# A planner's order placed anew, and two scan-kernel sums in one PSUM bank: an S4 layer with a feed-forward gate

## The chip, the cores and the metric

The kernel runs on one core of a Trainium2 chip. The core has a matrix engine (TensorE, PE in the views, with its weight loads as PEld), a vector engine (VectorE, DVE), a scalar engine (ScalarE, ACT), GpSimd (POOL) and SyncE (SP), which issues most of the transfers. Each runs its own instructions in program order; a semaphore holds an instruction until what it needs is there. SBUF is the on-chip memory, PSUM the banks into which PE accumulates, 2 KB per partition each. The metric is the time of one execution on the device in microseconds; the time before is the median of three runs.

## The reference

Both branches work on the normalised input; the result is the input plus their product. L is 2048, D 512, the state has 128 entries, and the hidden layer F is 1792 wide.

```python
xn = layernorm(u)
# branch A: an S4 convolution
logdA = dt * (A_re + 1j * A_im); dB = dt * (B_re + 1j * B_im)
P = exp(logdA[:, :, None] * arange(L))
K = einsum("dn,dnl,dn->dl", Cc, P, dB).real          # the scan kernel, 512 x 2048
y = irfft(rfft(pad(xn.T)) * rfft(pad(K)))[:, :L].T + xn * Dskip
# branch B: a feed-forward layer
g = silu(gelu(xn @ w1 + b1) @ w2 + b2)
out = u + y * g
```

## The kernel before

**Two stages.** The first, called the projection stage here, builds the scan kernel K and runs the feed-forward layer at the same time; in the trace it lasts from the start to about 392 us. The second does the convolution as small Fourier transforms written as matmuls, multiplies by the gate and adds the input. Only the first stage's code and order are touched.

**The feed-forward work.** The 2048 rows are four blocks of 512; the 14 tiles of the hidden layer are taken in two halves, so there are 56 steps j of one block and one tile. Each fp32 product is three matmuls, high times high, high times low and low times high. Per step: `F` is the first layer (two halves of six 128x512 matmuls, L250 to L252), `G` the gelu on ACT (L264), `H` the cast to the high part on ACT (L270), `R` the subtraction that gives the low part `hl` on DVE (L276), `S` the second layer (four parts of three matmuls, L289 to L291). `W`, `WB` load weights and `WS` splits them in high and low parts (ACT L233, DVE or POOL L235; the low part of the first layer's weight is `w1l`). For the later blocks the rows are normalised and turned here as well: `LS` and `LR` are statistics, `LC` the scaling of two row groups (DVE, L345), `TF` the transposes on PE (L361), `TH` and `TL` the split of the transposed rows into `xh` and `xl` (the latter on DVE, L376).

**The scan kernel.** K is built in 32 sets of 16 channels. Per set s: `KL` loads its numbers, `A` computes the phases (one bf16 matmul each for two halves, L593, into the `ph` bank), `B` rounds them to whole turns, on ACT (L601) or DVE (L603) as a flag in the order says, `C` takes the turns off (DVE, L607), `N` makes sines (ACT, L627 to L630), `Z` the sizes (POOL, a chain of seven operations, L616 to L621), `E` multiplies sizes and sines to the tables e1 and e2 (DVE, three steps: L642, L646, L648 and L649), `Q` sums over the state (64 fp32 matmuls of 128x32 by 128x64 in PE's records, L657), `U` copies the sum out of PSUM (ACT, L663), and `UD` stores it to DRAM (SP). `P` steps through the parameters that the sets need. The sums have one PSUM bank, tag `sm`, half filled. The tables have two buffers each.

**What sets the order.** `ORDER` (L48 to L128) is a string of tokens such as `F.24.0` or `E.11.2`; the kernel walks it from the first to the last and calls the function that the table `acts` (L735) names for each. Since the engines run in program order, the string fixes the order on every engine and every queue, and so which work stands ahead of a waiting instruction. The gelu and the sine need different tables in ACT, so an ACT_TABLE_LOAD stands wherever the string changes from the one to the other.

Of the kernel before, what the change touches and what calls it, by code (L numbers as in the profile page):

```python
# [48 lines left out]
WS.0.3 LD.0 LD.1 P.0 WS.1.0 WS.1.1 P.0 P.0 WS.1.2 G.0 F.1.0 LS.2.0 W.2 LS.3.1 H.0 R.0 WB.2 S.0.0 P.0  # L49
S.0.1 LS.3.0 LL.4 WS.1.3 P.0 WS.2.0 LL.5 W.3 F.1.1 WS.2.1 WB.3 S.0.2 LS.2.1 WS.2.2 G.1 WS.2.3 W.4 S.0.3  # L50
F.2.0 P.0 F.2.1 H.1 WS.3.0 R.1 WS.3.1 P.0 S.1.0 WS.3.2 WB.4 G.2 P.0 WS.4.0 S.1.1 W.5 WS.3.3 P.0 H.2
WS.4.1 P.0 WB.5 F.3.0 P.0 S.1.2 P.0 WS.4.2 LR.2 F.3.1 G.3 S.1.3 R.2 WS.5.0 WS.5.1 KL.0.0 F.4.0 WS.4.3.1
W.6 F.4.1 LC.2 H.3 LC.3 S.2.0 G.4 KL.0.1 TF.2.0 WB.6 BB A.0.0 TH.2.0 LS.5.0 R.3 S.2.1 KL.1.0 TF.2.1
LS.4.0 B.0.0.1 TH.2.1 TL.2.0 C.0.0 WS.6.0 S.2.2 S.2.3 H.4 TF.3.0 A.0.1 KL.1.1 WS.5.2 S.3.0 LS.5.1 WS.6.1
Z.0 B.0.1 P.0 P.1 TH.3.0 S.3.1 C.0.1 S.3.2 A.1.0 N.0.0 TL.2.1 S.3.3 KL.2.0 LD.2 TL.3.0 WS.6.2 B.1.0.1
C.1.0 R.4 F.5.0 TF.3.1 Z.1 LD.3 LS.4.1 N.0.1 A.1.1 B.1.1.1 F.5.1 S.4.0 WS.5.3.1 TH.3.1.1 C.1.1 G.5 S.4.1
E.0.0 S.4.2 S.4.3 E.0.1 TL.3.1 F.6.0 H.5 N.1.0 R.5 F.6.1 LR.4 N.1.1 F.7.0 E.0.2 G.6 A.2.0 B.2.0.1 S.5.0
KL.2.1 LC.5 H.6 F.7.1 S.5.1 P.1 LC.4 C.2.0 WS.6.3 LK.0 F.8.0 S.5.2 A.2.1 G.7 KL.3.0 H.7 B.2.1 P.1 F.8.1
R.6 G.8 KL.3.1 C.2.1 N.2.0 S.5.3 F.9.0 E.1.0 N.2.1 Q.0 A.3.0 S.6.0 S.6.1 S.6.2 F.9.1 Z.2 E.1.1 R.7 U.0
E.1.2 P.1 LD.5 B.3.0.1 LD.4 C.3.0 O.0.0 TF.4.0 KL.4.0 Q.1 Z.3 O.0.1 H.8 S.6.3 TH.4.0 O.0.3 G.9 A.3.1  # L60
S.7.0 TL.4.0 B.3.1.1 P.1 H.9 S.7.1 C.3.1 O.0.2 KL.4.1 TF.4.1 UD.0 LL.6 TH.4.1 R.8 F.10.0 F.10.1 E.2.0
S.7.2 S.7.3 N.3.0 E.2.1 A.4.0 TL.4.1 P.1 S.8.0 R.9 KL.5.0 U.1 E.2.2 N.3.1 B.4.0.1 G.10 OK.0 S.8.1 F.11.0
E.3.0 F.11.1 S.8.2 C.4.0 A.4.1 S.8.3 Q.2 G.11 B.4.1 H.10 UD.1 TF.5.0 E.3.1 E.3.2 LK.1 F.12.0 H.11 TH.5.0
C.4.1 A.5.0 KL.6.0 LS.6.0 F.12.1 B.5.0.1 S.9.0 S.9.1 R.10 N.4.0 G.12 S.9.2 TL.5.0 TF.5.1 P.1 N.4.1 C.5.0
KL.5.1 S.9.3 F.13.0 A.5.1 U.2 TH.5.1 F.13.1 R.11 S.10.0 P.1 B.5.1 Z.4 P.1 P.1 Q.3 C.5.1 N.5.0 TL.5.1
S.10.1 P.1 E.4.0 P.1 UD.2 U.3 F.14.0 N.5.1 H.12 E.4.1 S.10.2 KL.6.1 UD.3 S.10.3 R.12 E.4.2 Z.5 G.13 A.6.0
S.11.0 S.11.1 F.14.1 H.13 LK.2 E.5.0 R.13 E.5.1 LL.7 S.11.2 S.11.3 B.6.0.1 C.6.0 Q.4 Z.6 S.12.0 G.14
A.6.1 KL.7.0 F.15.0 E.5.2 P.1 S.12.1 LS.7.0 B.6.1 LS.7.1 F.15.1 P.2 C.6.1 S.12.2 A.7.0 S.12.3 G.15 LS.6.1
F.16.0 B.7.0 C.7.0 LR.6 N.6.0 A.7.1 S.13.0 LC.6 KL.8.0 S.13.1 U.4 H.14 R.14 P.1 H.15 F.16.1 N.6.1 LC.7
P.2 UD.4 E.6.0 B.7.1 R.15 S.13.2 LD.6 KL.7.1 C.7.1 F.17.0 Z.7 S.13.3 F.17.1 G.16 TF.6.0 O.1.0 O.1.2 Q.5  # L70
A.8.0 E.6.1 G.17 TF.7.0 S.14.0 TH.6.0 P.2 TH.7.0 E.6.2 O.1.1 U.5 O.1.3 H.16 KL.8.1 TL.6.0 TL.7.0 B.8.0
N.7.0 Z.8 S.14.1 S.14.2 N.7.1 S.14.3 F.18.0 OK.1 UD.5 C.8.0 TF.6.1 A.8.1 P.2 Q.6 F.18.1 S.15.0 B.8.1.1
R.16 TH.6.1 S.15.1 C.8.1 S.15.2 U.6 KL.9.0 S.15.3 E.7.0 H.17 E.7.1 S.16.0 W.7 S.16.1 G.18 WB.7 A.9.0
KL.9.1 F.19.0 F.19.1 R.17 E.7.2 B.9.0 TL.6.1 N.8.0 S.16.2 W.8 LD.7 S.16.3 N.8.1 G.19 S.17.0 TF.7.1 C.9.0
A.9.1 E.8.0 P.2 H.18 KL.10.0 TH.7.1 E.8.1 Q.7 B.9.1.1 UD.6 C.9.1 KL.10.1 H.19 D S.17.1 S.17.2 A.10.0
E.8.2 S.17.3 N.9.0 WB.8 F.20.0 TL.7.1 P.2 F.20.1 U.7 KL.11.0 N.9.1 R.18 Z.9 B.10.0 S.18.0 C.10.0 E.9.0
A.10.1 Q.8 G.20 F.21.0 XL.0 W.9 S.18.1 B.10.1 C.10.1 KL.12.0 N.10.0 E.9.1 N.10.1 WB.9 S.18.2 E.9.2 R.19
S.18.3 W.10 F.21.1 A.11.0 F.22.0 U.8 B.11.0 C.11.0 S.19.0 KL.11.1 G.21 H.20 S.19.1 A.11.1 S.19.2 UD.7
Z.10 B.11.1 P.2 P.2 F.22.1 UD.8 LK.3 S.19.3 R.20 F.23.0 WB.10 G.22 C.11.1 E.10.0 N.11.0 S.20.0 Z.11
A.12.0 F.23.1 N.11.1 S.20.1 Q.9 H.21 O.2.0 S.20.2 E.10.1 E.10.2 B.12.0 KL.12.1 F.24.0 H.22 C.12.0 A.12.1  # L80
U.9 S.20.3 F.24.1 B.12.1 O.2.1 R.21 R.22 G.23 S.21.0 S.21.1 Q.10 KL.13.0 O.2.3 F.25.0 O.2.2 E.11.0 F.25.1
C.12.1 E.11.1 KL.13.1 S.21.2 N.12.0 P.2 Z.12 KL.14.0 G.24 UD.9 P.2 H.23 N.12.1 U.10 R.23 P.2 E.11.2
S.21.3 P.2 Z.13 E.12.0 S.22.0 S.22.1 H.24 E.12.1 F.26.0 P.2 A.13.0 B.13.0 WS.7.0 Q.11 S.22.2 G.25 R.24
UD.10 C.13.0 F.26.1 S.22.3 A.13.1 WS.7.1 S.23.0 B.13.1.1 S.23.1 WS.8.0 S.23.2 C.13.1 KL.14.1 WS.7.2.1
# [1122 lines left out]
```

## Time and profile before

| | |
|---|---|
| median of the runs | 548.25 us (547.44 to 548.85) |
| profiled execution | 548.29 us |
| its span | 546.5 us |
| granted TensorE clock, mean | 0.996 |
| busy PE, DVE, ACT, POOL | 526.9, 463.9, 394.5, 279.1 us |
| ACT_TABLE_LOAD, all lines | 66 in the program, 1283 ns each |
| sum copies L663, 32 | 11.6 us |

In the page, busy time is the time in which an engine had an instruction running; PE's starts are recorded, its ends are modelled, and overlapping matmuls start less than their duration apart. In a row of a timeline stand the start, the duration, the engine, the line, the operation with its output and inputs, and in brackets the idle time before it with what ended it. In a row of groups stand the count, the busy time in us, the mean duration in ns, and the idle time ahead of the group with what ended it.

### The profile page before, as it was taken

Reading aid. Unit: us, or ns where it says so; the run is one execution under the profiler, and the core shown is the slowest. Engines: PE = TensorE matmul, PEld = TensorE weight load, DVE = VectorE, ACT = ScalarE, POOL = GpSimd, SP = SyncE. Lnnn points to the kernel's source line nnn. Section 1 sums busy time; section 2 is a strip of 40 time slices with the busy share of each in tenths; the row PEclk is TensorE's granted clock in tenths of the full one; section 3 lists DMA queues with packets and bytes.
Section 4 is the critical chain, followed back from the end, with each engine's and each line's share of the span. In section 5 each row is a group of like instructions: output and inputs, shape, how many; then the busy total and the mean of one; then the engine's idle time right before and its main releaser. Section 6 shows DMA issues by size and latency. Waiting matters only on the chain.

```text
span 546.5 us, 16626 instructions
## 1 busy us (share of the span) xinstructions
PE 526.9 (96%) x6999; PEld 421.2 (77%) x6999; DVE 463.9 (85%) x736; ACT 394.5 (72%) x570; POOL 279.1 (51%) x385
## 2 busy tenths in 40 slices
PE   8898999999999999999999999999999999999993
PEld 7666787778776777777777777777789998997971
DVE  6899989999999889999888797789557688787896
ACT  3777998898987899959799777889664573652430
POOL 5648379358968559996854296356301001203031
PEclk9999999999999999999999999999999999999998
DMA  8937526744385172837038412913547749361562
GB/s 228 315 124 227 196 83 221 237 150 146 121 245 180 33 237 90 270 102 198 18 110 263 123 47 84 188 45 103 204 160 221 136 127 189 120 194 67 182 208 93
DMA packets 88391, 85.85 MB, mean 157 GB/s; under 512 B 42134, under 2 KB 65050, under 8 KB 87292
## 3 DMA queue, kind: packets, MB, share of 16 engines
q1 hardware_dynamic: 79248, 66.43, 41.6%
q0 software_dynamic: 8768, 17.83, 10.6%
q8 instruction: 55, 0.90, 0.7%
q10 hardware_dynamic: 300, 0.53, 0.3%
q14 instruction: 20, 0.16, 0.1%
HBM read 51.22 MB, written 33.55 MB: 155 GB/s over the span
## 4 chain that ended last, share of the span: by engine, by line
PE 76%; DVE 17%; issue 2%; ACT 1%; POOL 1%; DMA 1%; DVEq 0%; ACTq 0%; POOLq 0%
PE s L913 11%; PE z L289 8%; PE z L290 7%; PE z L291 7%; PE f L250 7%; PE f L252 7%; PE f L251 7%; PE s L891 6%; PE sa L949 6%; PE kg L657 5%; PE ph L593 2%; DVE hl L276 2%; DVE ra L607 2%; DVE e L646 1%; PE y L989 1%
## 5 line engine op out<-in xcount | busy, mean ns | idle before, releaser
L619 POOL TENSOR_TENSOR mm<-mm,rc 128x32 f32<-128x32 f32 (+4 forms) x150 | 115.4, 769 | 11.8
L289 PE MATMUL z<-w2h,hh 128*128 128x512 f32 x224 | 97.8, 437 | 0.0
L250 PE MATMUL f<-xh,w1h 128*128 128x512 f32 x220 | 91.4, 416 | 0.0
L291 PE MATMUL z<-w2h,hl 128*128 128x512 f32 x224 | 88.4, 395 | 0.3 <-DVE hl L276 0.3
L252 PE MATMUL f<-xh,w1l 128*128 128x512 f32 x220 | 87.1, 396 | 1.7 <-DVE w1l L235 1.7
L290 PE MATMUL z<-w2l,hh 128*128 128x512 f32 x224 | 88.6, 395 | 0.0
L251 PE MATMUL f<-xl,w1h 128*128 128x512 f32 x220 | 86.7, 394 | 0.0
L913 PE MATMUL s<-X,mc 64*64 64x128 f32 x1536 | 60.4, 273 | 0.2 <-issue 0.2
L930 DVE TENSOR_TENSOR t<-s,uh 128x512 f32<-128x512 f32 x64 | 41.0, 684 | 22.8 <-ACT uh L921 22.6
L276 DVE TENSOR_TENSOR hl<-hf,hh 128x512 fp32r<-128x512 f32 x56 | 52.9, 948 | 4.6 <-ACT hh L270 4.6
L616 POOL COPY mm<-rc 128x32 f32<-128x32 f32 x30 | 13.4, 446 | 77.7 <-DVE e L649 53.4
L264 ACT ACTIVATE hf<-f,b1s 128x512 f32<-128x512 f32 x56 | 38.2, 688 | 20.4 <-DVE hl L276 11.7
L252 PEld LDWEIGHTS f<-xh,w1l 128*128 128x128 f32 x220 | 41.3, 188 | 12.9 <-DVE w1l L235 3.0
L289 PEld LDWEIGHTS z<-w2h,hh 128*128 128x128 f32 x224 | 42.5, 190 | 10.5 <-issue 1.0
L291 PEld LDWEIGHTS z<-w2h,hl 128*128 128x128 f32 x224 | 42.1, 188 | 10.7 <-DVE hl L276 0.7
L607 DVE SCALAR_TENSOR_TENSOR ra<-ra,ph 128x512 f32<-128x512 f32 x64 | 43.6, 681 | 7.5 <-ACT ra L601 6.5
L913 PEld LDWEIGHTS s<-X,mc 64*64 64x64 f32 x1536 | 44.5, 133 | 5.8 <-issue 1.7
L290 PEld LDWEIGHTS z<-w2l,hh 128*128 128x128 f32 x224 | 42.3, 189 | 8.3 <-DVE w2l L235 0.2
L250 PEld LDWEIGHTS f<-xh,w1h 128*128 128x128 f32 x220 | 41.5, 189 | 9.2 <-ACT hf L264 0.2
L251 PEld LDWEIGHTS f<-xl,w1h 128*128 128x128 f32 x220 | 41.4, 188 | 9.0
L921 ACT COPY uh<-s 128x512 f32<-128x512 f32 x32 | 18.7, 586 | 38.3 <-PE s L913 18.4
L642 DVE TENSOR_TENSOR e<-mm,ra 128x1024 f32<-128x1024 f32 x32 | 42.0, 1311 | 4.7 <-POOL pr_h L524 2.4
(184 smaller groups left out, 1161.1 us busy)
## 6 DMA issues: line engine op xcount, KB each, us to landing
x<-in_A_u_dram SPq DMA_DIRECT2D x8, 512.0 KB
xs<-x SPq DMA_DIRECT2D x8, 512.0 KB
xt_h<-xh POOLq DMA_DIRECT2D x4, 1024.0 KB, 5.5
xt_l<-xl POOLq DMA_DIRECT2D x4, 1024.0 KB, 7.6
kgd<-ko SPq DMA_DIRECT2D x32, 128.0 KB
za<-zo SPq DMA_DIRECT2D x4, 1024.0 KB
xh<-xt_h POOLq DMA_DIRECT2D x4, 1024.0 KB, 6.1
xl<-xt_l POOLq DMA_DIRECT2D x4, 1024.0 KB, 10.1
```

Source lines behind the costliest of these rows:

```text
L250: PE.matmul(p, wh[:, k, :], xh[:, k, :], start=(k == 0), stop=False)
L251: PE.matmul(p, wh[:, k, :], xl[:, k, :], start=False, stop=False)
L252: PE.matmul(p, wl[:, k, :], xh[:, k, :], start=False, stop=(k == KD - 1))
L276: V.tensor_sub(hl, hf, hh)
L289: PE.matmul(z, hh[:, s], wh, start=(f0 == 0 and not rows), stop=False)
L290: PE.matmul(z, hh[:, s], wl, start=False, stop=False)
L291: PE.matmul(z, hl[:, s], wh, start=False, stop=(f0 == FA - 1))
L607: V.scalar_tensor_tensor(ra[:, 0, c], ra[:, 1, c], MAGIC, p, op0=ALU.subtract, op1=ALU.subtract)
L619: GP.tensor_mul(mv[:, :, 0:3:2, w:2 * w], mv[:, :, 0:3:2, 0:w], rc[:, 2 + 2 * i:4 + 2 * i, :].rearrange("p j c -> p c j").unsqueeze(3).to_ ...
L642: V.tensor_mul(e1, m1.unsqueeze(1).to_broadcast([P, 2, CH, N1]), ra[:, :, :, :N1])
L913: PE.matmul(p[ka * 64:(ka + 1) * 64, r, o, :, jj], w, xf[b][h, c, :, k, :], start=(c == 0), stop=(c == 1), skip_group_check=True)
L930: V.tensor_mul(t, p[:, i, :, 1].unsqueeze(1).to_broadcast([P, 2, 2, P]), uh)
```

## The change

**One.** `gen_sum` is called for odd s only. It takes a bank of the shape [P, 2, DD, N2], which is the whole of 2 KB per partition, and runs over the tables of set s − 1 and of set s in one go, 128 matmul records with nothing else between. `gen_out` copies 128x512 elements once, from one bank to one tile `ko` (one buffer of double size where there were two), and `gen_keep` stores 256 KB at once. There are 16 `Q`, `U` and `UD` steps where there were 32. The tables of the even set are held until the pair's sum has run; they still have two buffers.

**Two.** The string `ORDER` is written anew from beginning to end, 1250 tokens where it had 1298; the 48 fewer are the even `Q`, `U` and `UD`. The work is the same otherwise, with two differences: 40 of the 64 roundings run on ACT and 24 on DVE, where 29 and 35 did, and there are 55 changes of the ACT table in the program where there were 66. Line numbers of the changed kernel are lower by 2.

```diff
@@ ORDER: three places of the new string, then the same of the old
+S.3.0 S.3.1 A.0.1 WB.6 WS.5.0 S.3.2 S.3.3 WS.5.1 LC.3 TF.3.0 B.0.1 C.0.1 P.0 P.1 WS.4.3.1 WS.6.0 TH.3.0
...
+A.15.0 N.13.1 N.14.0 E.13.0 Z.14 U.11 E.13.1 E.13.2 B.15.0 C.15.0 UD.11 S.26.2 WB.11 W.12 Z.15 H.27 R.27
+S.26.3 F.28.1 N.14.1 Q.13 G.28 F.29.0 WS.10.0 A.15.1 WS.11.0 WS.9.2 F.29.1 E.14.0 S.27.0 WB.12 WS.10.1
...
+U.23 G.47 F.48.0 A.27.1 KL.29.0 Q.25 N.26.0 B.27.1.1 C.27.1 S.45.2 S.45.3 N.26.1 N.27.0 R.46 S.46.0
...
-W.6 F.4.1 LC.2 H.3 LC.3 S.2.0 G.4 KL.0.1 TF.2.0 WB.6 BB A.0.0 TH.2.0 LS.5.0 R.3 S.2.1 KL.1.0 TF.2.1
@@ gen_size
-            for n in range(2):
-                GP.memset(par.tile([P, DD, N2], F32, tag="ko", name=f"ko_{n}", bufs=2)[:, 0, :1], 0.0)
+            GP.memset(par.tile([P, 2, DD, N2], F32, tag="ko", name="ko_")[:, 0, 0, :1], 0.0)
@@ gen_sum, gen_out, gen_keep
     def gen_sum(s):
-        e1, e2 = gen[s]["e"]
-        p = pss.tile([P, DD, N2], F32, tag="sm", name=f"kg{s}")
-        for d in range(DD):
-            for c in range(2):
-                for g in range(G):
-                    PE.matmul(p[g * N1:(g + 1) * N1, d, :], e1[:, c, g * DD + d, :], e2[:, c, g * DD + d, :],
-                              start=(c == 0), stop=(c == 1), skip_group_check=True)
+        p = pss.tile([P, 2, DD, N2], F32, tag="sm", name=f"kg{s}")
+        for n in range(2):
+            e1, e2 = gen[s - 1 + n]["e"]
+            for d in range(DD):
+                for c in range(2):
+                    for g in range(G):
+                        PE.matmul(p[g * N1:(g + 1) * N1, n, d, :], e1[:, c, g * DD + d, :], e2[:, c, g * DD + d, :],
+                                  start=(c == 0), stop=(c == 1), skip_group_check=True)
         gen[s]["p"] = p
     def gen_out(s):
-        gen[s]["ko"] = ko = par.tile([P, DD, N2], F32, tag="ko", name=f"ko{s}", bufs=2)
+        gen[s]["ko"] = ko = par.tile([P, 2, DD, N2], F32, tag="ko", name=f"ko{s}")
         A.copy(ko, gen[s]["p"])
     def gen_keep(s):
-        b, j = divmod(s, SPB)
-        SY.dma_start(kgd[b][:, j * DD * N2:(j + 1) * DD * N2], gen.pop(s)["ko"].rearrange("p a b -> p (a b)"))
+        b, j = divmod(s // 2, SPB // 2)
+        SY.dma_start(kgd[b][:, j * 2 * DD * N2:(j + 1) * 2 * DD * N2], gen.pop(s)["ko"].rearrange("p n a b -> p (n a b)"))
```

**Three places of the order.** The first is on DVE early in the stage, where the rows of the second block are scaled; `x_228` holds four groups of rows, `hl` is the low part of a step of the feed-forward layer, `xl` that of the transposed rows. Before:

```order
L340 SCALAR_TENSOR_TENSOR rs_358<-t_543,rs_358 128x4
L276 TENSOR_TENSOR hl_2_563<-hf_2_486,hh_2_505 128x512
L345 TENSOR_SCALAR x_228<-x_228,mv_357,rs_358 128x512 x4
L320 BN_STATS bst_0_615<-x_412 128x6
L321 BN_AGGR mv_613<-bst_0_615 128x2
L276 TENSOR_TENSOR hl_3_618<-hf_3_558,hh_3_591 128x512
L320 BN_STATS bst_0_630<-x_389 128x6
L321 BN_AGGR mv_613<-bst_0_630 128x2
L376 TENSOR_TENSOR xl_601<-xT_0_602,xh_600 128x4x128
```

And now:

```order
L338 SCALAR_TENSOR_TENSOR rs_380<-t_592,rs_380 128x4
L343 TENSOR_SCALAR x_228<-x_228,mv_379,rs_380 128x512 x2
L274 TENSOR_TENSOR hl_3_611<-hf_3_560,hh_3_585 128x512
L374 TENSOR_TENSOR xl_604<-xT_0_605,xh_603 128x4x128
L605 SCALAR_TENSOR_TENSOR ra_616<-ra_616,ph_0_614 128x512
L374 TENSOR_TENSOR xl_604<-xT_1_619,xh_603 128x4x128
L343 TENSOR_SCALAR x_228<-x_228,mv_379,rs_380 128x512 x2
```

Four scalings in a row have become two and two, with a low part, two `xl` subtractions and the first set's wrap between them; two statistics stand elsewhere.

The second place is on PE at the sums of the sets 10 and 11; `kg` is a sum, `e_10` and `e_11` are the tables, `z` the second layer's banks. Before, the two visits stand 36 rows apart; these are the rows of the later one:

```order
L252 MATMUL f_3_5_2453<-xh_1670,w1l_566 128x512
L593 LDWEIGHTS lh_2364
L593 MATMUL ph_0_2471<-cbs,lh_2364 128x512
L657 MATMUL kg_2480<-e_11_2376,e_11_2375 32x64 x32
L289 MATMUL z_2_2322<-w2h_329,hh_1_2296 128x512
L290 MATMUL z_2_2322<-w2l_330,hh_1_2296 128x512
```

And now:

```order
L289 MATMUL z_2_2255<-w2h_353,hl_2_2344 128x512
L655 MATMUL kg_2424<-e_10_2251,e_10_2250 32x64 x32
L655 MATMUL kg_2424<-e_11_2410,e_11_2409 32x64 x32
L591 LDWEIGHTS lh_2389
L591 MATMUL ph_1_2500<-cbs,lh_2389 128x512
L248 MATMUL f_3_5_2382<-xh_1700,w1h_636 128x512
```

Both sums fill one bank, and a phase matmul follows them directly.

The third place is on DVE at the same sets: what stands between the last table of set 11 and the first of set 12. Before:

```order
L276 TENSOR_TENSOR hl_2_2418<-hf_2_2318,hh_2_2412 128x512
L648 TENSOR_TENSOR e_11_2376<-mm_2221,ra_2142 128x16x32
L649 SCALAR_TENSOR_TENSOR e_11_2376<-mm_2221,ra_2142 128x16x32
L564 COPY al_2421<-pT_2423 128x128
L564 COPY rec_2420<-pT_2423 128x8x16
L642 TENSOR_TENSOR e_12_2441<-mm_2398,ra_2285 128x1024
```

And now:

```order
L646 SCALAR_TENSOR_TENSOR e_11_2410<-mm_2281,ra_2106 128x16x32
L601 TENSOR_SCALAR ra_2415<-ph_0_2402 128x512
L605 SCALAR_TENSOR_TENSOR ra_2415<-ra_2415,ph_0_2402 128x512
L274 TENSOR_TENSOR hl_3_2422<-hf_3_2341,hh_3_2377 128x512
L639 TENSOR_TENSOR e_12_2489<-mm_2320,ra_2301 128x1024
```

Before, the first table of set 12 took the buffer that the sum of set 10 had read 36 rows of PE earlier; now it takes the buffer that the pair's visit reads.

More of the change, by code (lines that the diff above doesn't have):

```diff
@@ L124 @@
[L124 to L127 removed]
+LD.0 W.2 P.0 P.0 P.0 LD.1 WS.0.3 WS.1.0 WS.1.1 WS.1.2 WS.1.3 WS.2.0 G.0 WB.2 LL.4 LL.5 W.3 F.1.0 F.1.1
+LS.2.0 H.0 R.0 S.0.0 G.1 H.1 WS.2.1 WS.2.2 WB.3 W.4 P.0 P.0 LS.3.1 LS.3.0 F.2.0 F.2.1 G.2 S.0.1 S.0.2
@@ new lines @@
+A.20.1 Z.20 S.35.0 H.36 E.19.1 B.20.1 C.20.1 N.20.0 F.38.1 A.21.0 R.36 KL.22.0 F.39.0 G.38 E.19.2
+B.21.0.1 ZA.0.1 KL.21.1 KL.22.1 F.39.1 F.40.0 C.21.0 A.21.1 ZA.0.3 H.37 R.37 Q.19 N.20.1 B.21.1.1
+KL.23.0 C.21.1 S.35.1 A.22.0 S.35.2 F.40.1 ZA.0.2 S.35.3 S.36.0 S.36.1 N.21.0 U.19 S.36.2 N.21.1 E.20.0
+E.20.1 Z.21 E.20.2 B.22.0.1 C.22.0 UD.19 H.38 G.39 Z.22 S.36.3 S.37.0 S.37.1 S.37.2 S.37.3 P.3 R.38
+E.21.0 F.41.0 G.40 ZG.0 F.41.1 SL1.0 H.39 P.3 P.3 A.22.1 B.22.1 C.22.1 P.3 F.42.0 H.40 S.38.0 S.38.1 P.3
@@ L128 @@
+KL.31.1 C.30.0 F.53.0 ZA.2.3 H.51 R.51 F.53.1 A.30.1 B.30.1.1 C.30.1 S.49.0 S.49.1 S.49.2 S.49.3 ST
+E.29.0 S.50.0 E.29.1 E.29.2 A.31.0 G.52 H.52 S.50.1 S.50.2 S.50.3 R.52 N.30.0 B.31.0.1 UD.27 C.31.0 Q.29
+G.53 A.31.1 B.31.1.1 C.31.1 N.30.1 S.51.0 E.30.0 E.30.1 S.51.1 S.51.2 S.51.3 S.52.0 F.54.0 F.54.1 F.55.0
+E.30.2 N.31.0 N.31.1 H.53 S.52.1 KL0 U.29 F.55.1 Z.31 E.31.0 ZG.2 S.52.2 E.31.1 E.31.2 R.53 UD.29 Q.31
+G.54 S.52.3 G.55 S.53.0 U.31 H.54 H.55 R.54 R.55 S.53.1 ZD.2 S.53.2 S.53.3 UD.31
 """
```

139 lines of the change are left out of this document (61 added, 78 removed).

## The prediction

> **What bounds the kernel now.** I read the page from above: busy shares and slices first, then the chain, then the busy time in two stages, the matrix engine's timeline around one sum visit, and the waits.
>
> ```profile
> span 546.5 us, 16626 instructions
> PE 526.9 (96%) x6999; PEld 421.2 (77%) x6999; DVE 463.9 (85%) x736; ACT 394.5 (72%) x570; POOL 279.1 (51%) x385
> PE   8898999999999999999999999999999999999993
> ...
> PE 76%; DVE 17%; issue 2%; ACT 1%; POOL 1%; DMA 1%; DVEq 0%; ACTq 0%; POOLq 0%
> ```
>
> TensorE (PE) is busy in every slice; the slices under 9 are the first and the third. The chain that ended last runs 76% over PE and 17% over VectorE (DVE). The next view cuts the span at the start, at 48 us and where the projection stage ends:
>
> ```profile
> 14.20:48.00 33.80, 28.94 (x123) 21.25 (x124) 31.59 (x73) 23.65 (x46) 21.06 (x34) 1.00 0.65 213
> 48.00:160.00 112.00, 111.89 (x1031) 87.28 (x1031) 105.91 (x171) 101.72 (x137) 77.32 (x109) 1.00 0.54 173
> 160.00:391.80 231.80, 229.87 (x2328) 176.18 (x2329) 202.25 (x264) 194.43 (x258) 150.28 (x186) 1.00 0.48 135
> 391.80:546.50 154.70, 144.63 (x3455) 125.73 (x3443) 114.48 (x202) 68.97 (x119) 22.16 (x26) 0.98 0.56 159
> ```
>
> Columns after the stretch and its length: busy us of PE, of its weight loads, of DVE, ACT (ScalarE), POOL (GpSimd), then the granted clock. Between 14.2 and 48 us PE idles 33.80 − 28.94 = 4.86 us, from 48 to 160 only 0.11, from 160 to 391.8 another 1.93. So the stage the change rewrites is bound by PE's own instructions, with one soft place at its start. Two things can move the time: PE's own work, and the waits the new order leaves. The last stretch keeps its code, so I give it no term.
>
> The sum is made against the profiled execution: 548.29 us, of which 546.5 is the span; the median of the runs is 548.25, the same for this purpose.
>
> **The change part by part.**
>
> *Two sums in one visit (16 visits for 32).* One clean visit of before, among ordinary matmuls, then one with a phase matmul (L593) right behind it, and the records by themselves:
>
> ```profile
> 318.76 0.39 PE L250 MATMUL f<-xh,w1h 128*128 128x512 f32 x1
> 319.00 0.40 PE L251 MATMUL f<-xl,w1h 128*128 128x512 f32 x1
> 319.23 0.39 PE L252 MATMUL f<-xh,w1l 128*128 128x512 f32 x1
> 319.55 1.10 PE L657 MATMUL kg<-e,e 128*32 128x64 f32 x64
> 320.58 0.50 PE L289 MATMUL z<-w2h,hh 128*128 128x512 f32 x1
> 320.92 0.40 PE L290 MATMUL z<-w2l,hh 128*128 128x512 f32 x1
> ...
> 68.09 0.39 PE L252 MATMUL f<-xh,w1l 128*128 128x512 f32 x1
> 68.41 1.10 PE L657 MATMUL kg<-e,e 128*32 128x64 f32 x64
> 69.44 0.39 PE L593 MATMUL ph<-cbs,lh 96*128 96x512 bf16 x1
> 69.48 0.58 PE L289 MATMUL z<-w2h,hh 128*128 128x512 f32 x1
> 69.90 0.40 PE L290 MATMUL z<-w2l,hh 128*128 128x512 f32 x1
> ...
> L657 PE MATMUL kg<-e,e x2048: 216/219/244, 68.4 to 392.0; 128*32 128x64 f32 x187
> ```
>
> Starts count, since ends are modelled. Ordinary 128x512 matmuls start 0.235 us apart (318.76, 319.00, 319.23). From the last one ahead of the visit to the second one behind it pass 320.92 − 319.23 = 1.69 us, where two ordinary steps would take 0.47: a visit costs 1.22. Its 64 records take 1.10 − 0.22 = 0.88 us from first start to last, 0.014 each. A doubled visit pays the edges once: 1.22 + 64 × 0.014 = 2.12, against 2 × 1.22 = 2.44. That is 0.32 saved, times 16: **−5.1 us**, all of it on the path, because PE is the bound. The other end is no saving at all, if going on to the second set's operands costs what entering a visit costs; no row shows two sets back to back. I take 5.1, because inside a visit the operands change at every record at 0.014 us.
>
> The Trainium skill, "TensorEngine Tiling (Array Packing)", Key Properties, says that changing the tiling mode drains TensorE. Were that a full drain, the entry would last the 0.39 of the matmul ahead; the row shows 0.32, and behind the visit the next matmul starts at 320.58, before the last record's modelled end at 320.65. So the trace bears out a partial drain. By a full one a visit would cost 0.39 + 1.10 + 0.34 − 0.47 = 1.36, a pair 2.25, and the saving would be 7.5 in place of 5.1; the measured starts decide.
>
> A phase matmul directly behind a visit hides in its edge: 69.90 − 68.09 = 1.81, where visit and phase matmul apart would be 1.69 + 0.235 = 1.93. The order has nine such neighbours where it had five: 4 × 0.12 = **−0.5**.
>
> *Copies, table loads, roundings.* The rows of before:
>
> ```profile
> L663 ACT COPY ko<-kg 128x256 f32<-128x256 f32 x32 | 11.6, 361 | 4.8 <-PE kg L657 4.6
> L921 ACT COPY uh<-s 128x512 f32<-128x512 f32 x32 | 18.7, 586 | 38.3 <-PE s L913 18.4 <-issue 10.2 <-ACT Z L960 7.3
> L264 ACT ACT_TABLE_LOAD x29 | 37.2, 1283 | 1.6 <-DVE hl L276 1.1
> L629 ACT ACT_TABLE_LOAD x24 | 30.8, 1283 | 0.4
> L603 DVE TENSOR_SCALAR ra<-ph 128x512 f32<-128x512 f32 x35 | 24.0, 685 | 12.8 <-PE ph L593 11.9
> ```
>
> ACT loses 16 copies: 32 × 0.361 become 16 × 0.586, the duration of another 128x512 copy, −2.2 us. With gelu and sine steps bunched, the program has 11 table loads fewer: 11 × 1.283 = −14.1. Eleven roundings move from DVE to ACT at 0.685 us: ACT +7.5, DVE −7.5. ACT ends 8.8 us lighter, DVE 7.5. I price all of it at nothing, because PE's idle from 48 us on is 2 us in 344: what hides it is PE's own queue. It is room, which the next terms use. Sixteen stores of 256 KB take the place of 32 of 128 KB on SyncE's (SP's) queue, the same bytes; nothing on PE's path waits for a store.
>
> *The start of the stage.* The four PE waits that make up the soft place:
>
> ```profile
> 17.41 0.40 PE L251 MATMUL f<-xl,w1h 128*128 128x512 f32 x1
> 19.32 0.50 PE L252 MATMUL f<-xh,w1l 128*128 128x512 f32 x1 [1.52 <-DVE w1l L235]
> ...
> 38.13 0.40 PE L291 MATMUL z<-w2h,hl 128*128 128x512 f32 x1
> 38.81 0.63 PE L361 MATMUL xT<-ident,x 128*128 128x128 f32 x4 [0.28 <-ACT hf L264]
> ...
> 39.96 0.39 PE L291 MATMUL z<-w2h,hl 128*128 128x512 f32 x1
> 40.92 0.66 PE L361 MATMUL xT<-ident,x 128*128 128x128 f32 x4 [0.57 <-ACT hf L264]
> ...
> 42.59 0.40 PE L291 MATMUL z<-w2h,hl 128*128 128x512 f32 x1
> 44.75 0.66 PE L361 MATMUL xT<-ident,x 128*128 128x128 f32 x4 [1.77 <-DVE xl L376]
> ...
> 37.81 3.79 DVE L345 TENSOR_SCALAR x<-x,mv,rs 128x512 f32<-128x512 f32 x4
> ```
>
> Beyond 0.235 each the starts are late by 1.68, 0.44, 0.73 and 1.93 us. The first waits for the low part of the first layer's second weight, which needs its load and a cast; the order brings neither forward, so 1.68 stays. The view names the gelu on ACT for the next two (it reads out the PSUM bank that the transposes L361 then write) and the `xl` subtraction on DVE for the last. That one stands behind the four scalings at 37.81, 3.79 us of DVE in one piece, though the block it belongs to needs only two of them. In the new order two scalings go ahead, then one `hl` and the two `xl` subtractions, and the other two scalings follow. That takes half the piece, 1.9 us, out of the way of the last wait of 1.93; the two of 0.44 and 0.73 I leave as they are, for ACT's gelu stays where it was against PE: **−1.9**. The ends are +1.9 (the second pair of scalings, moved behind, makes the next block's transposes late by what it saved) and −3.1 (all three waits go).
>
> *What the new order couples.* The tables e1 and e2 keep two buffers. Before, table building for set s+1 waited for the sum of s−1, long past. Now the sums of s−1 and s are one visit behind the tables of s, so the first table of the next even set waits for the whole pair: 15 places. DVE has other work between the last table of an odd set and the next first one; at the tightest, behind set 11, that is a rounding, a wrap and an `hl` subtraction.
>
> ```profile
> L607 DVE SCALAR_TENSOR_TENSOR ra<-ra,ph 128x512 f32<-128x512 f32 x64 | 43.6, 681 | 7.5 <-ACT ra L601 6.5
> L276 DVE TENSOR_TENSOR hl<-hf,hh 128x512 fp32r<-128x512 f32 x56 | 52.9, 948 | 4.6 <-ACT hh L270 4.6
> L642 DVE TENSOR_TENSOR e<-mm,ra 128x1024 f32<-128x1024 f32 x32 | 42.0, 1311 | 4.7 <-POOL pr_h L524 2.4 <-ACT ra L630 2.3
> ```
>
> That is 0.685 + 0.681 + 0.948 = 2.3 us, about one pair (2.12). Behind DVE's waiting table stand the wraps that ScalarE's sines need and the `hl` that PE's second layer needs. Also the sums have a single PSUM bank, now filled whole: a pair may not begin until the copy of the last one is done. The order leaves PE 7 matmuls (U.23 to Q.25: 1.6 us), 9 (U.29 to Q.31: 2.1) and 12 (U.11 to Q.13: 2.8) for it, with a copy of 0.586. Near the end POOL's two additions to the first kernel block, which wait for the block's load, now stand inside the size chain of a set (30), so tables come later if that load is late. I take **+1.0** for all of this: half of the 1.93 us that PE idles from 160 to 391.8 today, once more. The ends are 0 and the rival below.
>
> Sum: 548.3 − 5.1 − 0.5 − 1.9 + 1.0 = **541.8 us**.
>
> **Rivals.** (a) *Only the visits pay.* The early waits stay at 4.8 us because DVE's order there still holds a pair of scalings ahead of PE's transposes; everything else as above: 543.7. For it: DVE is busy 31.59 of 33.80 us there, so moving work within it frees little.
>
> (b) *The other side: DVE waits for the pairs.* At each of the 15 places PE's queue may reach the pair late, since PE runs in order and the pair stands behind its own matmuls. DVE is busy 202.25 of 231.80 us from 160 on, so it has little to catch up with. If each place held DVE for w us beyond its other work, the delay would be 15w less the 7.5 us of roundings it has lost; from 15w = 7.5 + 7.5 (the 5.6 of PE's work and the 1.9), w = 1.0 us, it eats the whole gain. At w = 1.25, somewhat more than half a pair, the time is 548.3 − 7.5 + 18.8 − 7.5 = 552.1. Against it: only the three tightest places have under 3 us of cover.
>
> (c) *The pairing saves nothing*, the second set's operands entering as a new visit does: 548.3 − 0.5 − 1.9 + 1.0 = 546.9, which can't be told from no change (0.3% is 1.6 us, about what measurement resolves here). A PE wait of 1.7 us at each of the three close copies would end in the same place, 541.8 + 5.1.
>
> (d) *More is gained*: the waits at the start nearly vanish (−3.1 further than 1.68) and ScalarE's and DVE's room removes the 1.93 us of idling after 160: 548.3 − 5.6 − 3.1 − 1.9 = 537.7.
>
> **How the numbers follow.** The forecast 0.45, (a) 0.20, (d) 0.13, (b) 0.15, (c) 0.07. Faster by over 0.3% is the forecast, (a) and (d): 0.78; same is (c): 0.07; slower is (b): 0.15. The range goes from 537.5, where (d) ends, to 548.0, past (c) and its neighbours, and leaves out (b) and the tail beyond (d), under 2 in 10 together. The likeliest case's own range is 540.0 to 543.5.
>
> **What would show it.** Right: 16 sum visits of 128 records, about 1.98 us from first start to modelled end (127 × 0.014 + 0.22 = 2.0), with 0.32 ahead and 0.34 behind; PE's idle from 14.2 to 48 us near 3.0; the copies near 0.59; 55 table loads; the last sum visit some 6.5 us earlier than the 392.0 us at which the last record of before starts. Wrong: an entry paid twice inside a visit; a wait of the first table line on the sums of more than 1 us at many places, with `ph` or `hl` waits of PE behind it; PE idle between 48 and 391 us of clearly more than 2 + 1 us; or a stretch after the projection stage that is longer than 154.7 us, which nothing here accounts for.

## The result, and the profile after

The changed kernel takes 556.03 us (555.32 to 556.79) where the kernel before took 548.35 in the same sessions: ratio 1.0144, 95% interval 1.0126 to 1.0162. It is slower by 7.7 us, outside the forecast range. The profiled execution took 555.65 us with a span of 553.8. One execution of a version below (e14) took 735 us at a granted clock of 0.655, and the ratios leave it out.

The page of the changed kernel, head, slices and chain:

```profile
span 553.8 us, 16537 instructions
PE 525.2 (95%) x6999; PEld 424.1 (77%) x6999; DVE 470.0 (85%) x725; ACT 388.0 (70%) x554; POOL 277.9 (50%) x384
PE   8898999999999889989999999999999999999993
...
PE 58%; DVE 25%; ACT 7%; issue 4%; SPq 2%; POOL 1%; DMA 1%; DVEq 0%; ACTq 0%; POOLq 0%
```

The chain runs 25% over DVE instead of 17, and there are soft slices in the middle of the stage. The same stretches as before, columns as in the prediction:

```profile
14.20:48.00 33.80, 29.96 (x126) 23.33 (x127) 29.69 (x67) 22.44 (x44) 15.66 (x27) 0.95 0.71 221
48.00:160.00 112.00, 110.06 (x967) 86.25 (x967) 106.05 (x168) 95.54 (x132) 73.83 (x104) 1.00 0.43 135
160.00:391.80 231.80, 223.10 (x2259) 173.38 (x2258) 204.56 (x256) 191.12 (x246) 153.47 (x195) 0.99 0.52 147
```

PE idles 1.94 us from 48 to 160 (0.11 before) and 8.70 from 160 to 391.8 (1.93 before). DVE is as busy as before in spite of 11 roundings fewer. The first full block of the last stage's first transform (64x128 matmuls) shows how late PE has become; the row of before, then of after:

```profile
393.71 2.05 PE L891 MATMUL s<-fc,in 64*128 64x128 f32 x30
```

```profile
400.18 2.06 PE L889 MATMUL s<-fc,in 64*128 64x128 f32 x32
```

That is 6.5 us, against the 5.6 that PE's own work was to save: some 12 us were lost ahead of this point, 8.6 of them as idle from 48 to 391.8 us. (The stage behind it took 0.8 us longer too, 153.6 for 152.8.) What PE waited for, in the whole execution (total us, times, longest); first the changed kernel, then the one before:

```profile
PE ph L591 <- DVE ra L605: 6.6, 8, 2.3
...
PE pT L559 <- DVE ra L605: 3.1, 2, 2.1
```

```profile
PE ph L593 <- DVE ra L607: 2.2, 4, 0.9
```

The two longest of these waits, in the timelines of PE:

```profile
182.69 0.39 PE L250 MATMUL f<-xh,w1l 128*128 128x512 f32 x1
185.22 0.30 PE L559 MATMUL pT<-ident,pr_ar 128*128 128x128 f32 x1 [2.14 <-DVE ra L605]
...
200.95 0.40 PE L289 MATMUL z<-w2h,hl 128*128 128x512 f32 x1
203.64 0.39 PE L591 MATMUL ph<-cbs,lh 96*128 96x512 bf16 x1 [2.29 <-DVE ra L605]
```

Both wait for the one phase bank, which the transposes of the parameters (L559) use too and which a wrap on DVE (L605) must read out first. What DVE did ahead of the second, and POOL beside it:

```profile
194.55 0.68 DVE L601 TENSOR_SCALAR ra<-ph 128x512 f32<-128x512 f32 x1
195.26 0.69 DVE L605 SCALAR_TENSOR_TENSOR ra<-ra,ph 128x512 f32<-128x512 f32 x1
195.87 2.17 DVE L643 TENSOR_TENSOR e<-mm,ra 128x1024 f32<-128x1024 f32 x1
197.95 3.03 DVE L645 TENSOR_TENSOR e<-mm,ra 128x512 f32<-128x512 f32 x1
200.91 0.68 DVE L646 SCALAR_TENSOR_TENSOR e<-mm,ra 128x512 f32<-128x512 f32 x1
...
202.90 0.68 DVE L605 SCALAR_TENSOR_TENSOR ra<-ra,ph 128x512 f32<-128x512 f32 x1
```

```profile
193.62 1.91 POOL L618 TENSOR_TENSOR mm<-mm,rc 128x512 f32<-128x512 f32 x1
...
197.06 2.12 POOL L233 TENSOR_TENSOR w1l<-ws,w1h 128x512 fp32r<-128x512 f32 x1
199.16 1.28 POOL L233 TENSOR_TENSOR w2l<-w2s,w2h 128x512 fp32r<-128x512 f32 x1
```

A table step of 128x512 that takes 0.68 us at its shortest took 3.03, and ended 0.5 us behind POOL's two subtractions. A rounding or a wrap, which reads PSUM, keeps its 0.68. The groups of the two larger table steps in the changed kernel follow; the same steps of before, L646 and L642, had means of 1412 and 1311 ns:

```profile
L643 DVE TENSOR_TENSOR e<-mm,ra 128x1024 f32<-128x1024 f32 x32 | 46.3, 1448 | 0.0
L639 DVE TENSOR_TENSOR e<-mm,ra 128x1024 f32<-128x1024 f32 x32 | 46.3, 1450 | 9.9 <-ACT ra L627 6.3 <-POOL pr_h L521 2.2 <-POOL mm L616 0.8
```

The first theory was then: **A**, the new order is to blame, with DVE slowed beside POOL (**A1**) or late by the places of its work (**A2**). The rival was **B**: the pairing is to blame, because tables wait for pairs.

### The profile page after: what moved, and what is told of

Same layout as the page of the kernel before. It is cut to its first block, busy times and chain, and to the rows that moved or that the text cites. A ratio compares the mean times of both kernels' runs of the same rounds, so it can differ in the third digit from the quotient of the medians.

```text
span 553.8 us, 16537 instructions
## 1 busy us (share of the span) xinstructions
PE 525.2 (95%) x6999; PEld 424.1 (77%) x6999; DVE 470.0 (85%) x725; ACT 388.0 (70%) x554; POOL 277.9 (50%) x384
## 4 chain that ended last, share of the span: by engine, by line
PE 58%; DVE 25%; ACT 7%; issue 4%; SPq 2%; POOL 1%; DMA 1%; DVEq 0%; ACTq 0%; POOLq 0%
PE s L911 11%; PE s L889 6%; PE sa L947 6%; PE z L287 5%; PE z L288 5%; PE z L289 5%; PE f L248 4%; PE f L250 4%; PE f L249 4%; DVE e L639 3%; DVE e L643 3%; DVE ra L605 3%; PE kg L655 3%; DVE hl L274 2%; DVE e L645 2%
## 5 line engine op out<-in xcount | busy, mean ns | idle before, releaser
L616 POOL TENSOR_TENSOR mm<-mm,rc 128x32 f32<-128x32 f32 (+4 forms) x150 | 105.8, 705 | 11.7
L287 PE MATMUL z<-w2h,hh 128*128 128x512 f32 x224 | 96.2, 429 | 0.0
L248 PE MATMUL f<-xh,w1h 128*128 128x512 f32 x220 | 93.3, 424 | 0.0
L928 DVE TENSOR_TENSOR t<-s,uh 128x512 f32<-128x512 f32 x64 | 41.1, 684 | 23.9 <-ACT uh L919 23.6
L613 POOL COPY mm<-rc 128x32 f32<-128x32 f32 x30 | 14.7, 492 | 85.0 <-DVE e L646 71.0
L639 DVE TENSOR_TENSOR e<-mm,ra 128x1024 f32<-128x1024 f32 x32 | 46.3, 1450 | 9.9 <-ACT ra L627 6.3
L605 DVE SCALAR_TENSOR_TENSOR ra<-ra,ph 128x512 f32<-128x512 f32 x64 | 43.7, 683 | 10.6 <-ACT ra L599 9.8
L274 DVE TENSOR_TENSOR hl<-hf,hh 128x512 fp32r<-128x512 f32 x56 | 47.5, 856 | 4.5 <-ACT hh L268 4.5
L289 PEld LDWEIGHTS z<-w2h,hl 128*128 128x128 f32 x224 | 42.3, 189 | 10.2
L643 DVE TENSOR_TENSOR e<-mm,ra 128x1024 f32<-128x1024 f32 x32 | 46.3, 1448 | 0.0
```

Source lines behind the costliest of these rows:

```text
L248: PE.matmul(p, wh[:, k, :], xh[:, k, :], start=(k == 0), stop=False)
L274: V.tensor_sub(hl, hf, hh)
L287: PE.matmul(z, hh[:, s], wh, start=(f0 == 0 and not rows), stop=False)
L289: PE.matmul(z, hl[:, s], wh, start=False, stop=(f0 == FA - 1))
L605: V.scalar_tensor_tensor(ra[:, 0, c], ra[:, 1, c], MAGIC, p, op0=ALU.subtract, op1=ALU.subtract)
L616: GP.tensor_mul(mv[:, :, 0:3:2, w:2 * w], mv[:, :, 0:3:2, 0:w], rc[:, 2 + 2 * i:4 + 2 * i, :].rearrange("p j c -> p c j").unsqueeze(3).to_ ...
```

## The experiments

**The two halves of the change, each alone (e1, e2).** e1 keeps the old order and pairs the sums; the first table of an even set then has to stand behind the pair. e2 keeps the new order and puts the single visits back.

```diff
 # e1: ORDER of before without the even Q, U, UD; for example
-E.12.0 S.22.0 S.22.1 H.24 E.12.1 F.26.0 P.2 A.13.0 B.13.0 WS.7.0 Q.11
+S.22.0 S.22.1 H.24 Q.11 E.12.0 E.12.1 F.26.0 P.2 A.13.0 B.13.0 WS.7.0
 # e2: gen_sum, gen_out, gen_keep of before; the new ORDER with
+Q.s (s even, some 2 us of PE's work behind E.s.2) U.s UD.s
```

> The order of before, with the sums of two sets in one visit as in the changed kernel; a sum or the first table of the next even set is moved by a few places where the pair would otherwise need a buffer that is not free. Theory A (the new order is to blame: with it DVE comes late for the phase bank, and pairing by itself pays what it saves on PE): 543 to 546 us, the 5.1 us of the visits less a us or two of new waits. Theory B (the pairing is to blame: the first table of an even set waits for a whole pair, and DVE's tables come in bursts): 551 us or more, with waits of the tables on the sums.

> The new order, with one visit per set as before; the sum of an even set stands some 2 us of PE's work behind its last table. Theory A (the order): 558 to 562 us, the changed kernel's 556.0 plus up to 5.1 for the visits. Theory B (the pairing): 550 us or less, since the tables of a set are free again one set earlier.

Measured: e1 566.84 us, ratio to before 1.0326 (1.0297 to 1.0355); e2 571.60, ratio 1.0405 (1.0378 to 1.0432). e1 lies where B put it, e2 above what A gave for it; neither theory said that both halves lose by themselves. In e1 the waits of DVE and PE read:

```profile
DVE e L636 <- PE kg L652: 23.9, 10, 3.7
...
PE ph L588 <- DVE ra L602: 12.3, 13, 2.7
```

Tables wait for sums ten times, 23.9 us in all, and PE for wraps behind them. So the rival that I had given 0.15 is a real mechanism, in the old order. The new order places tables and sums so that in its own trace such a wait comes once, of 0.4 us. e2 then shows that this order is built for pairs; part of its loss may be my placing of the single visits, on whose tables PE waits 5.5 us in all, 2.9 at the longest.

**Is it the waiting for pairs? (e8, e15).** Here the doubled visit reads the odd set's tables twice. The even sets' sums are left out, PE's work stays, and no table of an even set waits for a pair.

```diff
         for n in range(2):
-            e1, e2 = gen[s - 1 + n]["e"]
+            e1, e2 = gen[s]["e"]
```

> The order of before with the even sums, copies and stores dropped and nothing else moved; the doubled visit reads the odd set's tables twice, so the even set's are read by nobody and the output is that of other sums. PE does the same work as in e1, but no table has to wait for a pair. If e1's 566.8 us came from tables waiting for pairs (23.9 us of DVE's waits there): 543 to 546 us, the 5.1 us of the visits and nothing lost. If it came from something else in the doubled visit or its copy: over 555 us.

> The changed kernel with the doubled visit reading the odd set's tables twice, so that no table waits for a pair; the output is that of other sums. If the new order has taken the pairing's cost out (0.4 us of direct waits in its trace): 555 to 556.5 us. If the pairs still hold DVE back in ways that the waits do not name: 551 us or less.

Measured: e8 546.55, ratio 0.9960 (0.9946 to 0.9974), against e1's 566.84: some 20 us were the waits for pairs, with the seven tables and four sums that e1 had to move for them. The pairs then gain 2.3 of their 5.1 us; PE's phase matmuls wait 3.3 us on wraps there (2.2 before), 1.2 at the longest. e15, the same edit in the new order: 556.72, ratio 1.0144 (1.0127 to 1.0161), the changed kernel's own. So in the new order the waiting for pairs costs nothing that can be measured, and B is out for the changed kernel.

**POOL beside DVE (e3, e4, e13).** e3 and e4 leave POOL's size chains out behind the second set, in the changed kernel and in the one before. e13 keeps POOL occupied, with the same buffers, by operations that read nothing (they don't wait for a set's numbers either, as the chain does):

```diff
 # e3, e4
+        if s > 1:
+            gen[s]["mm"] = sizes[s % 2]
+            return
 # e13
+        if s > 1:
+            for _ in range(3):
+                GP.memset(mm, 0.5)
+            gen[s]["mm"] = mm
+            return
```

> The changed kernel without POOL's size chains of the sets 2 to 31: their tables are made from the sizes of the sets 0 and 1, so the output is that of other sizes. DVE's work keeps its instructions. Theory A1 (DVE is late because its tables run beside POOL's size chains and take longer there): table steps back at their shortest, about 1.21 and 0.68 us, PE's idle between 48 and 400 us down to a few us, 541 to 546 us. Theory A2 (DVE is late by the places of its work alone): still over 552 us.

> The kernel before without the size chains of the sets 2 to 31, the same omission. It has 1.9 + 0.1 us of PE idle behind 48 us, so there is little to win: 545.5 to 548 us by either theory. By A1 the kernel above falls below it by about the 5 us of the visits; by A2 it stays above it.

> The changed kernel in which POOL sets the whole size tile of the sets 2 to 31 to a constant, three times over, in place of the chain of seven operations: about as long on POOL, with the same waits and buffers, but reading nothing from SBUF; the output is that of other sizes. If DVE's table steps are slow because POOL reads the memory beside them: tables near 1.25 and 0.7 us as without the chains, and 543 to 546 us. If the gain of the run without size chains (543.4) came from POOL being free for its other work: 551 to 556 us.

Measured: e3 543.37, ratio 0.9898 (0.9876 to 0.9919); e4 546.48, ratio 0.9952 (0.9934 to 0.9969); e13 542.00, ratio 0.9878 (0.9860 to 0.9896). Without the chains the changed kernel gains 12.7 us and the one before 2.6 (549.05 in that session), and the changed one is 3.1 us the faster. e3's profiled execution has the low clock near the start, 0.95 from 14.2 to 48 us as in the changed kernel, so that low clock is no part of this gain. The group of POOL's settings and of two table steps in e13, and its third stretch:

```profile
L614 POOL MEMSET mm<- 128x1536 f32 x90 | 125.4, 1395 | 110.0 <-DVE e L651 106.7
...
L648 DVE TENSOR_TENSOR e<-mm,ra 128x1024 f32<-128x1024 f32 x32 | 42.2, 1317 | 0.0
L644 DVE TENSOR_TENSOR e<-mm,ra 128x1024 f32<-128x1024 f32 x32 | 39.8, 1245 | 6.8 <-ACT ra L632 4.3 <-POOL pr_h L522 1.9 <-POOL mm L614 0.3
```

```profile
160.00:391.80 231.80, 231.06 (x2470) 181.26 (x2469) 182.39 (x261) 195.77 (x253) 125.59 (x107) 1.00 0.55 159
```

POOL still works 125.59 us in this stretch (153.47 in the changed kernel), yet DVE needs 182.39 us instead of 204.56 for five instructions more, and PE idles 0.7 us instead of 8.7. The cost is not that POOL is busy, but that it reads beside DVE's two-input steps. A1 holds. The Trainium skill, "SBUF — State Buffer", SBUF: two separate sides, says that a DVE operation with two SBUF inputs and a GpSimd operation that reads SBUF take turns on a shared pair of ports, whichever starts first holding it to its end; the 3.03 us step beside two subtractions, and the steps that shrink beside settings, agree with it.

How much DVE's steps were stretched shows where the chains are left out. Busy us of all of a kind, from the groups of DVE; the parameter steps are L504 to L549 of the changed kernel:

| | before | e4, no chains | changed | e3, no chains | e13, settings |
|---|---|---|---|---|---|
| table steps, 128 | 142.0 | 125.8 | 146.4 | 127.9 | 128.8 |
| `hl` subtractions, 56 | 52.9 | 40.7 | 47.5 | 38.5 | 40.2 |
| parameter steps, 96 | 38.4 | 31.5 | 47.5 | 32.7 | 47.0 |

The chains lengthen the three kinds by 35.3 us before and by 42.3 in the changed kernel. The 7 us more are about what the 11 roundings had freed on DVE. Settings give back the tables and the `hl`, but not the parameter steps, many of which have one input: beside settings such steps are stretched as well. The scalings of the rows (L343) took 0.97 us on the mean in e13 and 0.66 in e3. So what is said of reads holds for the two-input steps.

**Can the waits be mended by places? (e5)** Six local edits of the new order, for example:

```diff
-G.26 H.26 E.12.1 E.12.2 B.14.0 LK.3 KL.15.0 R.25 KL.15.1 W.10 S.24.2 S.24.3 C.14.0 P.2 A.14.1
+G.26 H.26 R.25 E.12.1 E.12.2 B.14.0 LK.3 KL.15.0 KL.15.1 W.10 S.24.2 S.24.3 S.25.0 S.25.1 S.25.2 S.25.3 C.14.0 P.2 A.14.1
-S.30.3 R.31 R.32 C.18.0
+S.30.3 R.31 C.18.0 R.32
```

> The changed kernel with six places of its order mended, one for each of the longest waits of PE behind 100 us: a parameter step behind a wrap instead of ahead of it, two transposes later, second-layer parts ahead of a phase matmul, a low part behind a wrap. Work is the same. If PE's waits are a matter of places: the 10 us of these six waits come back but for a few, 546 to 550 us. If DVE as a whole is too slow beside POOL: the waits move on to the next phase matmul, over 553 us.

Measured: 552.63, ratio 1.0068 (1.0051 to 1.0084). Of the 10 us 3.4 came back. Part of the rest moved on: a phase matmul at 224.07 us now waits 1.90 us for a wrap, where the changed kernel has no wait of a quarter of a microsecond or more between 204 and 247 us. The time is between the two expectations, nearer to that of a slow DVE.

**The division of the roundings (e6, e9, e10).** Only the flag of the `B` steps differs:

```diff
 # e6: all on ACT      e9: as before (29 ACT, 35 DVE)      e10: all on DVE
-B.13.0 ... B.13.1.1
+B.13.0.1 ... B.13.1.1
```

> The changed kernel with all 64 roundings on ACT: DVE loses 24 x 0.688 = 16.5 us, ACT gets as much. If the amount of DVE's work makes the wraps late: 549 to 553 us. If it is the chain by which a rounding must wait for the tables of two sets before, and ACT's gelu waits behind it: 556 us or more.

> The changed kernel with the roundings of before: each half of each set on the engine that had it there (29 on ACT, 35 on DVE; 27 of 64 change sides). All roundings on ACT cost 22 us more, so if a rounding on ACT is dear because it waits for tables with the gelus behind it: 551 to 554 us. If the new flags fit the new order better than the old ones: 557 us or more.

> The changed kernel with all 64 roundings on DVE: DVE gains 40 x 0.688 = 27.5 us of work, ACT loses as much. If only the side on ACT is dear: under 553 us. If DVE's work is what makes the wraps late: 560 us or more. With the run of all roundings on ACT at 578 a result over 560 here says that the division in the new order is near its best.

Measured: e6 578.07, ratio 1.0528 (1.0506 to 1.0550); e9 564.96, ratio 1.0293 (1.0277 to 1.0308); e10 570.18, ratio 1.0373 (1.0346 to 1.0399). My reading of e6, that ACT alone is the dear side, fell with e9. In e6 DVE's wraps wait for ACT's roundings:

```profile
DVE ra L602 <- ACT ra L596: 45.4, 36, 4.2
...
ACT ra L596 <- DVE e L643: 19.5, 12, 6.6
PE ph L588 <- DVE ra L602: 17.2, 13, 3.9
```

A rounding on ACT waits for the tables of the set two before, whose buffer it writes, and ACT's gelus wait behind it; on DVE it lengthens DVE's own queue. Either way the phase matmul comes late. Of the four divisions tried the new flags are the best for the new order. So roundings moved off DVE were not room, as I had priced them; they were needed.

**The clock (e7), and the two mends together (e11, e12).** PE's first wait, for the low part of a weight at 17.5 us, is filled with eight matmuls into a bank that is unused then:

```diff
+            if (v, f) == steps[1] and k == 0:
+                q = pss.tile([P, TB * P], F32, tag="sm", name="fill")
+                for _ in range(8):
+                    PE.matmul(q, wh[:, 0, :], xh[:, 0, :], start=True, stop=True, skip_group_check=True)
             PE.matmul(p, wl[:, k, :], xh[:, k, :], start=False, stop=(k == KD - 1))
```

> The changed kernel with eight matmuls of 128x512 into the unused sum bank where PE waits at 17.5 us for the low part of a weight; nothing reads them. If the clock of about 0.5 between 20 and 23.4 us follows from PE's idling there: clock 1.00 in these slices and 1.7 us less, 554.3 us. If it has another reason: the same slices stay at 0.5 and the time at 556 us or a little over.

Measured: 553.48, ratio 1.0086 (1.0071 to 1.0101), 2.5 us under the changed kernel. Three of PE's stretches between 19 and 23 us, columns as above, the third from the end being the granted clock; first the changed kernel, then two of them with the filling:

```profile
19.00:20.00 1.00, 0.22 (x1) 0.22 (x2) 1.00 (x2) 0.74 (x2) 0.83 (x3) 1.00 0.49 186
20.00:21.00 1.00, 1.00 (x4) 0.75 (x4) 1.00 (x2) 0.97 (x2) 0.92 (x2) 0.54 0.90 221
22.00:23.00 1.00, 1.00 (x4) 0.81 (x3) 1.00 (x3) 0.00 (x0) 0.92 (x2) 0.50 1.10 320
```

```profile
20.00:21.00 1.00, 1.00 (x6) 0.82 (x5) 0.97 (x3) 0.97 (x3) 0.84 (x3) 1.00 0.79 264
22.00:23.00 1.00, 1.00 (x5) 0.78 (x5) 1.00 (x3) 0.70 (x2) 0.92 (x2) 1.00 0.95 328
```

That looks like the filling's work, but it isn't shown. e3 and e13 have no filling and the same order and wait at this place; their first stretch:

```profile
14.20:48.00 33.80, 30.00 (x126) 23.33 (x127) 29.57 (x66) 22.43 (x44) 15.89 (x26) 0.95 0.70 225
```

```profile
14.20:48.00 33.80, 29.40 (x130) 22.89 (x131) 30.96 (x68) 23.95 (x47) 17.79 (x28) 1.00 0.73 230
```

Of the nine profiled executions with the new order and no filling, PE waits 1.7 to 1.9 us there in all; four have a clock of 0.50 to 0.64 from 20.2 to 23 us (the changed kernel, e3, e10, e15), and five have 1.00 (e2, e5, e6, e9, e13). The three with the filling (e7, e11, e12) have 1.00. The gain in time is measured; in the profiled executions 0.8 us of it is less idling of PE between 48 and 160 us (1.15 for 1.94), and how much the filling does for the clock stays open.

> The six mended places and the eight filling matmuls together. If they are worth what each was alone (3.4 and 2.5 us): 550 us. If the filling only moved where the clock drops: 552 us or more.

> The same with the roundings of before. By the first reading of the flags 546 to 549 us, by the second 552 or more.

Measured: e11 552.09, ratio 1.0064 (1.0038 to 1.0090), no better than the mends alone; in e5's profiled execution the same wait, of 1.7 us, was not followed by a low clock, so there the filling had nothing to win. e12 565.40, ratio 1.0294 (1.0269 to 1.0318): the old flags cost 13.3 us here and 8.9 in e9, and both end at 565.

**Pairs only where nothing waited (e14, e16).** Five pairs in the kernel before, copies and stores per set. e14 stores the even set at its old place where that is possible; e16 later, mostly next to the odd set's store.

```diff
+    PAIRS = (1, 3, 13, 15, 31)
     def gen_sum(s):
+        sets = (s - 1, s) if s in PAIRS else (s,)
-        p = pss.tile([P, DD, N2], F32, tag="sm", name=f"kg{s}")
+        p = pss.tile([P, 2, DD, N2], F32, tag="sm", name=f"kg{s}")
```

> The kernel before with five pairs only, (0,1), (2,3), (12,13), (14,15) and (30,31), behind which no table had to wait for a pair in the run with the old order; copies and stores per set as before. If a pair without a wait is worth its 0.32 us: 5 x 0.32 = 1.6 us, 547 us. If the later sums cost by themselves: 549 us or more.

> The kernel before with the same five pairs, but the stores of the even sets moved behind as well, next to those of the odd ones: in the run before this one a phase matmul waited 3.80 us for its load behind an early store on SP's queue. If that store was the loss: 546.5 to 548 us, 1.6 us under before less a little. If pairing costs where no table waits: 549 us or more.

Measured: e14 552.67, ratio 1.0070 (1.0051 to 1.0089). In the profiled execution its loss has one place, in the timeline of PE:

```profile
225.34 0.61 PE L590 MATMUL ph<-cbs,lh 96*128 96x512 bf16 x1 [3.80 <-DMA lh<-pcd]
```

It waits for the load of set 17's numbers, and SP's timeline says why that was late:

```profile
199.20 1.28 SPq L218 DMA_DIRECT2D w2s<-in_B_w_dram  x1
216.17 0.33 SPq L668 DMA_DIRECT2D kgd<-ko  x1
...
219.50 0.65 SPq L576 DMA_DIRECT2D lh<-pcd  x1
```

From 200.5 us SP issued nothing until 216.17, when the store of set 12, whose copy I had moved behind, could go; the loads stood behind it. e16 moves the stores: 548.65, ratio 0.9997 (0.9979 to 1.0015). The expected 1.6 us are not to be seen: the interval ends 1.2 us under the kernel before, so the whole gain is out, and a smaller one neither shown nor refuted. No version here that does all the work beats the kernel before.

## Why the prediction was wrong, by its steps

- **The visits, −5.1: right.** A clean pair of the changed kernel:

```profile
127.36 0.40 PE L289 MATMUL z<-w2h,hl 128*128 128x512 f32 x1
127.69 1.99 PE L655 MATMUL kg<-e,e 128*32 128x64 f32 x128
129.61 0.50 PE L287 MATMUL z<-w2h,hh 128*128 128x512 f32 x1
129.95 0.39 PE L288 MATMUL z<-w2l,hh 128*128 128x512 f32 x1
```

  129.95 − 127.36 − 0.47 = 2.12 us, the 2.12 worked out. Three more pairs cost 2.11 or 2.12. The second set's operands enter without an edge of their own, so a full drain, by which it would be 2.25, and rival (c), are out. The last pair is an exception, below. With a phase matmul behind it a pair cost 2.24, that matmul included, so the −0.5 was right as well.
- **Copies, table loads, roundings, priced at nothing: this step failed.** The sizes of the copies (0.577 us) and the 55 table loads came as forecast. But I counted 7.5 us fewer on DVE and 8.8 on ACT as room. DVE's busy time from 14.2 to 391.8 is 340.3 us after and 339.7 before: other steps took back what the roundings gave. POOL's chains stretch DVE's steps by 7 us more in the new order, parameter steps above all. And I took PE's own queue as the cover, while PE must wait for each wrap before the next phase matmul can have the one bank. In the new order that queue no longer covers a late wrap: PE's waits for wraps are 9.7 us where they were 2.2. A stretch of 35.3 us cost the kernel before 2.6 (e4), one of 42.3 cost the changed kernel 12.7 (e3).
- **The start, −1.9: wrong in size.** PE's idle from 14.2 to 48 us fell from 4.86 to 3.84 us, 1.0 of the 1.9. The four scalings did split into 1.81 and 1.97 us, but the first pair started at 41.49 us instead of 37.81, and its first scaling took 1.35 us (0.53 at the shortest) while POOL's L618 ran beside it. So the transposes still waited, 1.54 us, until 0.1 us behind that scaling's end; the view names the gelu, which had been done for 0.8 us. The second pair held up a wrap (0.88). The wait for the weight stayed, 2.0 us beyond the usual step, and the clock fell to a half behind it, 1.6 us that no term had.
- **What the new order couples, +1.0: the term that was mis-sized.** Direct waits of tables for pairs are 0.4 us (e15: none that costs). The price was elsewhere: PE idles 10.6 us from 48 to 391.8 us, 8.6 more than before, mostly for wraps (2 + 1 was the most that the prediction allowed for), and two stretches of low clock cost 3.2 us together (each 128x512 step 0.427 us instead of 0.235 over some 3.5 us), and the last pair's gap 1.0. Less the 1.0 gained at the start, that is 11.8 of the 12.1 us lost (6.5 + 5.6). DVE's steps stretched beside POOL are the cause of most of it: without the chains' reads PE idles 0.7 us (e13) or 2.7 (e3) from 160 to 391.8 us where it idles 8.7. That e13's 542.0 is near the forecast's 541.8 is chance, for the forecast kept the chains. Without chains on both sides the change gains 3.1 us, not the forecast 6.5.
- **Rival (b)** had the right side and a mechanism that exists (e1, e8), but not in this order. Its bound, 15 us in all, is what e1 went far over with ten waits of 2.4 us on the mean.
- The two sets of the final pair stand 1.03 us apart in the changed kernel, because the second one's tables end late. POOL's two additions within the size chain of set 30, which I had listed, have a part in it. In the trace POOL stands 9.5 us for the kernel block's load, from 370.9 to 380.4 us, so its chain for set 31 runs from 384.1 to 391.3 us, beside the tables of both sets, and five table steps there take 2.5 us more than at their shortest. In e13 POOL waits 7.1 us for that load, but no chain runs beside those tables, and the gap is gone. No run moved the additions alone.

What stays open: how much of e2's loss is my placing; why five pairs without waits show no gain; why a wait of 1.9 us is followed by a low clock in some executions and not in others; and which of the new order's places, beyond those that e5 mended, leave a wrap without cover.

## What to carry to other kernels

A saving on the busiest engine is worth its size only while every resource with one buffer, here the phase bank, is handed back in time; price a new order by the chain that hands it back, not by each engine's sum. When durations are taken over from a trace, ask which of them are stretched by a neighbour: steps on VectorE that read SBUF have no fixed price beside GpSimd, and an order that shifts them against each other changes the sum. Pairing work that shares double buffers takes their slack away, so buffers, order and pairing have to be changed together, and each alone can lose more than both.

## What the runs showed of the hardware

- A table step of 128x512 on DVE took 0.68 us at its shortest and up to 3.03 beside two subtractions on POOL; steps that read PSUM kept 0.68. POOL settings of 1.395 us, which read nothing, left the larger table steps at 1.25 and 1.32 us on the mean, where the chains made them 1.45.
- One-input scalings of 128x512 took 0.53 us at the shortest, and 0.97 on the mean in the run with settings, so it is the two-input steps that settings leave alone.
- The granted clock fell to 0.5 for about 3.5 us behind waits of PE of 1.9 and 2.3 us, but not behind one of 2.1 us at 183 us of the same execution. The first of these waits was followed by a low clock in four of nine profiled executions, so its length alone does not decide.
